# Forgetting attention and two MoE layers on one core: a new table of times for the order of the attention's operations and of the weight work between them

## The chip, the core and the metric

The kernel is one program on one core of a Trainium2 chip. The metric is the time of one execution on the device in microseconds (us); the median of several executions is compared. The core's engines work side by side, each on its own list of instructions in a fixed order: PE (TensorE, matrix products), DVE (VectorE), ACT (ScalarE), POOL (GpSimd), and SP (SyncE), whose queue issues most transfers. An instruction that waits holds up everything behind it on its own engine.

## What is computed

Three stages, each feeding the next; all data are fp32.

```python
# 32 heads (4 batches x 8 heads), S = 576 positions, D = 64
scores = (q @ k^T) / sqrt(D)
cum    = cumsum(log(clip(f, 1e-4, 1)))
scores = where(causal, -1e9, scores + cum[:, :, :, None] - cum[:, :, None, :])
attn   = exp(scores - max(scores)); attn = attn / (sum(attn) + 1e-9)
x      = attn @ v                             # to 2304 tokens x 512
x      = softplus(x @ w_in) @ w_out           # first MoE, 512 -> 2048 -> 512
out    = (sigmoid(x @ w_gate) * (x @ w_val)) @ w2_out   # second MoE, 512 -> 1536 -> 512
```

## The kernel before, in words

Products are made in fp32r from a high and a low half of each operand (three products for one), so copies to a high half and subtractions for a low half (names ending in `h` and `l`) follow nearly every step.

**Attention** works on 16 pairs of heads, `p` = 0 to 15. For one pair PE makes the scores: `s4` (tile `s{p}_4`, L225, all 128 rows) and `s3`, `s1`, `s2` (L239, two heads side by side on 64 rows each). DVE takes minimum and mask out of PSUM (`minimum`, L246), ACT makes the exponential and its sum (`exp`, L251). PE transposes the result in seven groups `t0` to `t6` (`transposes`, L270; two PSUM banks in turn), ACT copies each group out to its high half (`evac_h`, tile `PTh`, L292), DVE subtracts for the low half (`evac_l`, tile `PTl`, L296), and PE multiplies with the values (`pv`, L345) into an accumulator for each head, `x{p}_0` and `x{p}_1`, each one PSUM tile of 1024 columns. `pv(0, j)` stands for the j-th block of columns of the first head.

The sums go their own way: POOL adds the small constant (`rinv_a`, L301), DVE takes the reciprocal (`rinv`, L304), PE transposes the nine columns of it into the first 128 columns of the accumulator `x{p}_0` (`rinv_t`, L308), ACT copies these nine rows out (`rinv_b`, tile `rt_sb`, L312), SP writes them to DRAM and reads them back spread over rows (`rinv_c`, L316, tile `rd`; `rinv_d`, L322, tile `rb`). At the end ACT and DVE take the accumulators out (`out_a`, L355, tile `bs`; `out_b`, L360, tile `xs`), POOL multiplies with `rb` (`out_c`, L363), and SP writes the pair's result with three transfers (`out_d`, L370 to L372).

`Attention.run` sorts all operations of all pairs by one number each: 9 times the pair plus a number from the table WHEN (pair 0 takes START, pair 15 takes END). Engines keep that order; nothing else decides it. In the same sorted list stand the preparation of the first MoE's weights and its first work:

- STEPS and LATE_STEPS: steps of `Weights.op` by class. 0 LOAD (SP, L498, tile `raw`), 1 SCALE (ACT, L506, tile `w`), 2 SHIFT (DVE, L520), 3 LOW (DVE, L522), 4 SIGN (DVE, L524), 5 HI (ACT, L511), 6 LO (POOL, L514). The jobs are `wi0`, `wo0`, `wi1`, and so on.
- X_STEPS: loading the first 512 tokens (DVE L569, POOL L570), PRODUCTS: the first products `h0`, `h1` of the first MoE, UNITS: their softplus and split.

**The first MoE** then runs 80 units (5 token tiles x 16 blocks). A unit is PE's product `h` (12 matmuls, L577 to L579), ACT's softplus to `L` (L614) and copy to `gh` (L625), DVE's subtraction to `gl` (L626), and PE's product `o` (12 matmuls). One unit's `o` follows the next one's `h`. In the first tile each unit also ticks the weight chain on by two steps of each class.

Of the kernel before, what the change touches and what calls it, by code (L numbers as in the profile page):

```python
# [21 lines left out]
class Attention:  # L22
# [342 lines left out]
    def out_d(self, R, p):  # L365
# [13 lines left out]
        ("load_q",): 1.4836, ("qh",): 2.2896, ("load_k",): 3.0664, ("ql",): 3.3216, ("decay_rows",): 3.4423,  # L379
        ("kh",): 7.4598, ("kl",): 7.8752, ("scores", 4): 10.3002, ("load_v",): 11.0784, ("minimum", 4): 11.5052,  # L380
        ("scores", 3): 11.5060, ("minimum", 5): 14.0106, ("minimum", 3): 14.3071, ("scores", 1): 15.9948,
        ("minimum", 7): 16.2237, ("minimum", 1): 16.2736, ("minimum", 8): 16.3365, ("minimum", 0): 16.4858,
        ("exp", 4): 16.5320, ("exp", 5): 16.9077, ("scores", 2): 18.0750, ("exp", 3): 18.0806, ("exp", 7): 19.0711,
# [13 lines left out]
    START = {
        ("scores", 1): -280.1001, ("minimum", 7): -271.8782, ("minimum", 0): -231.7545, ("minimum", 8): -193.8316,
        ("minimum", 1): -187.7875, ("exp", 7): -173.7344, ("exp", 0): -167.8599, ("scores", 4): -157.5166,
        ("minimum", 4): -141.6254, ("scores", 2): -110.2675, ("exp", 4): -105.8996, ("minimum", 6): -105.0800,  # L400
        ("minimum", 2): -102.9800, ("scores", 3): -95.1511, ("exp", 6): -85.4990, ("exp", 2): -83.7134,
        ("exp", 8): -70.4444, ("exp", 1): -64.2521, ("minimum", 5): -59.3775, ("exp", 5): -50.7529,
        ("load_v",): -48.7810, ("transposes", 1): -35.9211, ("minimum", 3): -29.2582, ("exp", 3): -25.6744,
        ("transposes", 3): -19.5338, ("evac_h", 1): -8.3683, ("evac_h", 3): -6.7983, ("evac_l", 1): -1.6145,
        ("evac_l", 3): 10.5292, ("v_high",): 17.2888, ("rinv_a",): 18.4155, ("v_low",): 19.8820,
        ("transposes", 0): 20.3326, ("evac_h", 0): 21.2188, ("rinv",): 21.7400, ("evac_l", 0): 22.6562,
        ("transposes", 2): 22.8149, ("rinv_t",): 23.1362, ("evac_h", 2): 24.0607, ("rinv_b",): 24.3022,
        ("evac_l", 2): 24.5160, ("pv", 0, 0): 24.9295, ("transposes", 5): 24.9438, ("pv", 0, 2): 25.7706,
        ("transposes", 4): 25.7715, ("pv", 0, 4): 26.8567, ("evac_h", 5): 27.3271, ("evac_l", 5): 27.7081,
        ("evac_h", 4): 28.2950, ("evac_l", 4): 28.6956, ("transposes", 6): 28.8354, ("pv", 0, 3): 29.6197,  # L410
        ("rinv_c",): 29.8827, ("pv", 0, 1): 29.9362, ("evac_h", 6): 30.0612, ("evac_l", 6): 30.1210,
        ("pv", 1, 0): 30.1250, ("pv", 1, 2): 30.2412, ("out_a", 0): 32.2739, ("out_b", 0): 32.4826,
        ("rinv_d",): 33.9341, ("pv", 1, 4): 34.5831, ("pv", 1, 3): 35.1273, ("pv", 1, 1): 35.7267,
        ("out_a", 1): 36.1134, ("out_b", 1): 36.5534, ("out_c",): 40.4646, ("out_d",): 46.2880}
    END = {
        ("load_k",): -5.3504, ("load_q",): -2.6412, ("kh",): 3.0783, ("decay_rows",): 4.0312, ("qh",): 4.4239,
        ("load_v",): 4.8618, ("kl",): 5.5915, ("ql",): 7.9462, ("scores", 4): 10.6000, ("scores", 3): 11.4633,
        ("minimum", 4): 11.8140, ("minimum", 5): 13.7921, ("minimum", 3): 13.9946, ("exp", 4): 15.4472,
        ("exp", 5): 15.6399, ("scores", 1): 16.2743, ("minimum", 7): 16.8650, ("minimum", 1): 16.9709,
        ("exp", 1): 17.1448, ("minimum", 0): 17.2852, ("minimum", 8): 17.5873, ("exp", 0): 17.9416,  # L420
        ("exp", 8): 19.1832, ("scores", 2): 19.2862, ("v_high",): 19.8660, ("v_low",): 20.2468,
        ("minimum", 6): 20.6005, ("exp", 3): 21.0068, ("minimum", 2): 22.1762, ("exp", 7): 23.4705,
        ("exp", 6): 24.5954, ("exp", 2): 24.6233, ("transposes", 1): 24.7520, ("evac_h", 1): 24.7985,
        ("evac_l", 1): 25.3933, ("rinv_a",): 27.9027, ("transposes", 0): 29.1264, ("transposes", 3): 30.9396,
        ("evac_h", 0): 31.4482, ("evac_h", 3): 32.7310, ("evac_l", 0): 47.1260, ("rinv",): 56.8557,
        ("transposes", 2): 57.3718, ("evac_l", 3): 62.0535, ("transposes", 5): 63.6052, ("evac_h", 5): 77.8251,
        ("evac_h", 2): 79.9965, ("evac_l", 2): 85.0192, ("transposes", 4): 87.7824, ("rinv_t",): 92.6295,
        ("pv", 0, 0): 99.8173, ("evac_l", 5): 108.0667, ("transposes", 6): 108.0726, ("pv", 0, 4): 111.3911,
        ("pv", 0, 3): 111.7383, ("evac_h", 4): 113.9795, ("pv", 0, 2): 115.1968, ("evac_l", 4): 125.8108,
        ("evac_h", 6): 127.6254, ("pv", 0, 1): 132.0278, ("out_a", 0): 132.6996, ("rinv_b",): 152.9427,  # L430
        ("rinv_c",): 153.0347, ("evac_l", 6): 156.2053, ("pv", 1, 0): 166.3307, ("pv", 1, 3): 187.2979,
        ("pv", 1, 2): 201.4660, ("out_b", 0): 212.3156, ("pv", 1, 4): 218.5856, ("pv", 1, 1): 220.1616,
        ("rinv_d",): 225.0768, ("out_a", 1): 292.1891, ("out_b", 1): 319.5476, ("out_c",): 321.9904,
        ("out_d",): 353.5322}
# [543 lines left out]
LATE_STEPS = [(-16.2008, 2), (-15.8847, 5), (-14.7068, 3), (-12.1943, 6), (-3.5317, 1), (-3.1825, 0), (2.5760, 3),  # L978
              (13.9908, 4), (15.5227, 2), (26.5633, 5), (50.6610, 1), (56.3007, 3), (61.7718, 6), (69.1876, 2),
              (69.7883, 4), (72.7702, 3), (75.4909, 0), (90.6667, 0), (148.9901, 4), (149.6626, 0), (177.5320, 5),  # L980
              (208.1786, 4), (237.2145, 6), (441.5471, 0)]
X_STEPS = [-54.8771, -48.5972, -35.8360, -23.0657, -14.2717, -5.4128, -3.8231, 6.3816]
PRODUCTS = [43.6366, 61.7680]
UNITS = [100.4307, 349.1830]
# [198 lines left out]
```

## Time and profile before

| | us |
|---|---|
| median of 3 executions | 1013.31 (1012.34 to 1013.75) |
| profiled execution | 1011.11 |
| its span from first to last instruction | 1009.3 |
| PE busy | 1000.1 |
| DVE busy | 592.9 |
| ACT busy | 509.9 |
| POOL busy | 154.9 |

The profile is of one execution. Its span leaves out 1.8 us of the execution that stand before the first and behind the last instruction. PE is busy nearly all the time, so a microsecond that PE waits is close to a microsecond of time; where the other engines wait costs nothing by itself.

### The profile page before, as it was taken

Reading aid. Unit: us, or ns where it says so; the run is one execution under the profiler, and the core shown is the slowest. Engines: PE = TensorE matmul, PEld = TensorE weight load, DVE = VectorE, ACT = ScalarE, POOL = GpSimd, SP = SyncE. Lnnn points to the kernel's source line nnn. Section 1 sums busy time; section 2 is a strip of 40 time slices with the busy share of each in tenths; the row PEclk is TensorE's granted clock in tenths of the full one; section 3 lists DMA queues with packets and bytes.
Section 4 is the critical chain, followed back from the end, with each engine's and each line's share of the span. In section 5 each row is a group of like instructions: output and inputs, shape, how many; then the busy total and the mean of one; then the engine's idle time right before and its main releaser. Section 6 shows DMA issues by size and latency. Waiting matters only on the chain.

```text
span 1009.3 us, 15958 instructions
## 1 busy us (share of the span) xinstructions
PE 1000.1 (99%) x5614; PEld 883.9 (88%) x5614; DVE 592.9 (59%) x1210; ACT 509.9 (51%) x1085; POOL 154.9 (15%) x170
## 2 busy tenths in 40 slices
...
GB/s 176 162 162 161 165 164 132 108 156 207 208 64 207 251 260 205 182 177 168 238 83 248 226 185 338 212 247 214 219 269 209 248 223 208 188 265 216 217 137 63
DMA packets 114700, 196.10 MB, mean 194 GB/s; under 512 B 14702, under 2 KB 38398, under 8 KB 114620
## 3 DMA queue, kind: packets, MB, share of 16 engines
...
q8 instruction: 45, 0.74, 0.3%
...
## 4 chain that ended last, share of the span: by engine, by line
PE 91%; DMA 3%; DVE 2%; ACT 2%; POOL 1%; issue 1%; SPq 0%; POOLq 0%; ACTq 0%; DVEq 0%
PE z L577 9%; PE z L579 9%; PE z L578 9%; PE x L345 6%; PE h L577 6%; PE h L578 6%; PE h L579 6%; PE s L239 5%; PE t L270 5%; DMA raw_wo<-in_moe_w_out_dram 3%; PE oY L577 2%; PE oY L578 2%; PE oY L579 2%; PE s L225 2%; PE oX L577 2%; PE oX L578 2%
## 5 line engine op out<-in xcount | busy, mean ns | idle before, releaser
L577 PE MATMUL z<-three,three 128*128 128x384 f32 x456 | 153.3, 336 | 0.2
L579 PE MATMUL z<-three,three 128*128 128x384 f32 x456 | 152.9, 335 | 0.0
L578 PE MATMUL z<-three,three 128*128 128x384 f32 x456 | 152.6, 335 | 0.0
L626 DVE TENSOR_TENSOR gl<-L,gh 128x512 fp32r<-128x512 f32 (+1 forms) x80 | 51.1, 638 | 117.5 <-ACT gh L625 113.5
L614 ACT ACTIVATE L<-h 128x512 f32<-128x512 f32 (+1 forms) x80 | 44.3, 554 | 143.7 <-PE h L579 143.7
L577 PEld LDWEIGHTS z<-three,three 128*128 128x128 f32 x456 | 85.6, 188 | 2.7 <-DVE raw L887 0.5
L578 PEld LDWEIGHTS z<-three,three 128*128 128x128 f32 x456 | 85.6, 188 | 1.4
L251 ACT ACTIVATE P<-P,m 128x256 f32<-128x256 f32 (+3 forms) x144 | 83.7, 584 | 5.0 <-DVE m L246 4.7
L579 PEld LDWEIGHTS z<-three,three 128*128 128x128 f32 x456 | 85.6, 188 | 0.0
L246 DVE CUSTOM_DVE_ANT_0 P<-s,mask 128x256 f32<-128x256 f32 (+3 forms) x144 | 69.4, 515 | 10.6 <-PE s L239 9.4
L296 DVE TENSOR_TENSOR PTl<-t,PTh 128x512 fp32r<-128x512 f32 (+2 forms) x112 | 68.2, 619 | 5.4 <-ACT PTh L292 5.0
L874 ACT COPY bl<-z 128x384 f32<-128x384 f32 x36 | 17.3, 480 | 102.3 <-PE z L579 102.3
L886 DVE TENSOR_TENSOR raw<-z,bh 128x384 f32<-128x384 f32 x36 | 20.1, 558 | 76.5 <-PE z L579 76.5
L879 DVE TENSOR_TENSOR raw<-z,p 128x384 f32<-128x384 f32 x18 | 10.0, 558 | 92.9 <-PE z L579 79.0
L292 ACT CAST PTh<-t 128x512 fp32r<-128x512 f32 (+2 forms) x112 | 58.0, 539 | 9.5 <-PE t L270 7.0
L270 PE MATMUL t<-ident,P 128*128 128x128 f32 x400 | 61.9, 279 | 0.4 <-DVE PTl L296 0.4
L345 PE MATMUL x<-PTh,V 128*128 128x256 f32 (+2 forms) x224 | 59.1, 316 | 0.8 <-ACT rt_sb L312 0.8
L908 ACT CAST gh<-raw 128x384 fp32r<-128x384 f32 x72 | 33.5, 514 | 48.6 <-DVE raw L891 47.2
L345 PE MATMUL x<-PTl,V 128*128 128x256 f32 (+2 forms) x224 | 53.9, 292 | 0.0
L270 PEld LDWEIGHTS t<-ident,P 128*128 128x128 f32 x400 | 45.1, 140 | 7.6 <-DVE r L304 3.6
L727 DVE TENSOR_TENSOR l<-fw,sh 128x512 fp32r<-128x512 f32 x60 | 40.7, 687 | 13.9 <-ACT sh L726 7.1
L625 ACT CAST gh<-L 128x512 fp32r<-128x512 f32 (+1 forms) x80 | 46.2, 578 | 2.5
...
## 6 DMA issues: line engine op xcount, KB each, us to landing
...
```

The lines of the kernel that those rows point to most:

```text
L239: nc.tensor.matmul(ps[h][:, a:a + N], L[o], r[o, 0:N], start=j == 0, stop=j == n - 1)
L246: self.nc.vector.tensor_tensor_reduce(P, src, mask, -0.125, 3e38, op0=ALU.add, op1=ALU.min, accum_out=R["m"][:, t:t + 1])
L251: self.nc.scalar.activation(P, P, AF.Exp, bias=R["m"][:, t:t + 1], scale=-1.0, accum_out=R["sum"][:, t:t + 1])
L270: nc.tensor.transpose(ps[:, 128 * n:128 * n + 128], R["P"][:, o:o + 128], self.ident)
L292: self.nc.scalar.copy(d, s)
L296: self.nc.vector.tensor_sub(l, s, h)
L345: nc.tensor.matmul(R["acc%d" % h][:, o:o + n], v, t[:, col:col + n], start=j == 0 and w == 0, stop=j == 1 and w == 1)
L577: nc.tensor.matmul(ps, ah, bh, start=start and i == 0, stop=False, **how)
L578: nc.tensor.matmul(ps, ah, bl, start=False, stop=False, **how)
L579: nc.tensor.matmul(ps, al, bh, start=False, stop=stop and i == n - 1, **how)
L625: nc.scalar.copy(gh, s)
L626: nc.vector.tensor_sub(gl, s, gh)
```

## The change

Only numbers change: WHEN, START, END, STEPS, LATE_STEPS, X_STEPS, PRODUCTS, UNITS, the time at which the pools of the first MoE are opened, and that of the softplus table's preload. The operations, their sizes and their buffers are the same. Of the tables a few entries stand for all:

```diff
@@ WHEN (of 62 entries)
-        ("transposes", 0): 22.8649, ("transposes", 1): 23.1190, ("evac_h", 0): 23.3248, ("evac_l", 0): 23.4902,
...
-        ("evac_l", 4): 29.2931, ("evac_h", 6): 30.1251, ("evac_l", 6): 30.1452, ("pv", 0, 2): 30.2200,
-        ("pv", 0, 3): 30.6720, ("pv", 0, 1): 32.1361, ("pv", 1, 0): 32.9471, ("pv", 1, 2): 33.3019,
-        ("rinv_b",): 33.6120, ("out_a", 0): 34.7767, ("pv", 1, 4): 34.7925, ("pv", 1, 3): 35.3192,
...
+        ("transposes", 5): 29.8251, ("rinv_t",): 30.0728, ("pv", 0, 0): 30.1572, ("transposes", 4): 30.2737,
+        ("pv", 0, 4): 30.4394, ("rinv_b",): 30.4528, ("evac_h", 5): 30.5384, ("evac_l", 5): 30.6828,
...
+        ("evac_l", 6): 31.9050, ("rinv_c",): 32.2991, ("pv", 0, 3): 33.1511, ("pv", 0, 2): 34.6838,
@@ the list of other steps
-        others += [(end + 10.2872, open_pools), (end + 500, W.alone)]
+        others += [(end + 12.4572, open_pools), (end + 500, W.alone)]
...
-        others += [(end + 60.7767, lambda: nc.scalar.preload_act_table_set("softplus"))]
+        others += [(end + 73.1642, lambda: nc.scalar.preload_act_table_set("softplus"))]
```

What this does to the engines' lists is seen in the lists themselves. The first place is ACT in the middle of the attention, where pair 7's transposes are taken out (`t7_5`, `t7_4`) and pair 8's exponentials run (`P8`). Before:

```order
L292 CAST PTh_195<-t7_5_1747 128x2x256
L251 ACTIVATE P8_1579,sum8_1581<-P8_1579,m8_1580 128x256
L292 CAST PTh_195<-t7_4_1762 128x384
...
L292 CAST PTh_195<-t7_6_1790 128x2x128
...
L292 CAST PTh_195<-t8_0_1836 128x512
L292 CAST PTh_195<-t8_1_1842 128x512
L312 COPY rt_sb7_1871<-x7_0_1753 9x128
L251 ACTIVATE P9_1770,sum9_1772<-P9_1770,m9_1771 128x576
```

The same place in the changed kernel:

```order
L251 ACTIVATE P8_1605,sum8_1607<-P8_1605,m8_1606 128x256
L312 COPY rt_sb7_1789<-x7_0_1776 9x128
L292 CAST PTh_195<-t7_5_1770 128x2x256
L251 ACTIVATE P8_1605,sum8_1607<-P8_1605,m8_1606 128x256
L292 CAST PTh_195<-t7_4_1783 128x384
L251 ACTIVATE P8_1605,sum8_1607<-P8_1605,m8_1606 128x384
L292 CAST PTh_195<-t7_6_1816 128x2x128
```

The copy of `rt_sb` moved from behind the copies of the next pair's `t0` and `t1` to ahead of the copy of its own pair's `t5`. It does so in pairs 1 to 13; in pair 14, too, it now stands ahead of the copy of `t5`.

The second place is PE behind the scores `s3` of pair 9, with pair 7's products with the values (`x7_0`) and pair 8's transposes. Before:

```order
L239 MATMUL s9_3_1_1801<-nb1_133,one_135 128x512
L345 MATMUL x7_0_1753<-PTh_195,V7_1597 128x320
L345 MATMUL x7_0_1753<-PTl_196,V7_1597 128x320
L345 MATMUL x7_0_1753<-PTh_195,V7_1597 128x256
L345 MATMUL x7_0_1753<-PTl_196,V7_1597 128x256
L270 MATMUL t8_0_1836<-ident_184,P8_1579 128x128 x4
L270 MATMUL t8_1_1842<-ident_184,P8_1579 128x128 x4
```

And in the changed kernel:

```order
L239 MATMUL s9_3_1_1822<-nb1_133,one_135 128x512
L270 MATMUL t8_0_1836<-ident_184,P8_1605 128x128 x4
L270 MATMUL t8_1_1847<-ident_184,P8_1605 128x128 x4
L345 MATMUL x7_0_1776<-PTh_195,V7_1619 128x256
L345 MATMUL x7_0_1776<-PTl_196,V7_1619 128x256
L345 MATMUL x7_0_1776<-PTh_195,V7_1619 128x320
L345 MATMUL x7_0_1776<-PTl_196,V7_1619 128x320
```

The two groups of transposes moved ahead of four products with the values; all other PE instructions of a pair keep their places relative to one another.

The third place is ACT at the end of the attention, where the last pair's transposes (`t15_2`, `t15_4`, `t15_6`) and the first unit's softplus and copy (`L0`, `gh0`) stand. Before:

```order
L292 CAST PTh_195<-t15_2_3214 128x512
L614 ACTIVATE L0_3267<-h0_3200 128x512
L625 CAST gh0_3269<-L0_3267 128x512
L292 CAST PTh_195<-t15_4_3251 128x384
L292 CAST PTh_195<-t15_6_3264 128x2x128
L355 COPY bs15_3287<-x15_0_3255 64x576
L312 COPY rt_sb15_3289<-x15_0_3255 9x128
```

And in the changed kernel:

```order
L292 CAST PTh_195<-t15_2_3226 128x512
L312 COPY rt_sb15_3259<-x15_0_3219 9x128
L614 ACTIVATE L0_3261<-h0_3181 128x512
L625 CAST gh0_3263<-L0_3261 128x512
L292 CAST PTh_195<-t15_4_3251 128x384
L292 CAST PTh_195<-t15_6_3272 128x2x128
```

The last pair's copy moved to ahead of the first unit's softplus. SP's transfers follow it: the write of `rd15` moves ahead of the load of the weights `wo5`, the two reads of `rb15` ahead of the load of `wi6`. The three writes of pair 15's result still stand ahead of the load of `wo6` in both kernels. On DVE two weight steps of each pair now stand together behind the minimum of `s3` and ahead of the low half of `t0`; before they were spread over the pair.

## Rows read from the trace of the kernel before

**Rows 1.** Part 1 of the page: busy time, share of the span, instructions.
```profile
PE 1000.1 (99%) x5614; PEld 883.9 (88%) x5614; DVE 592.9 (59%) x1210; ACT 509.9 (51%) x1085; POOL 154.9 (15%) x170
```
**Rows 2.** Busy time of engines by window, in the middle of the attention; clock after POOL.
```profile
100.00:175.00 75.00, 75.00 (x629) 65.44 (x627) 69.92 (x200) 71.17 (x197) 62.37 (x59) 1.00 0.56 156
```
**Rows 3.** The chain of waits, pairs 2 and 7: start, us, what.
```profile
48.57 1.15 PE s L225 x8
...
101.74 0.90 PE s L239 x8
...
104.33 1.15 PE s L225 x8
```
**Rows 4.** Waits of PE: us in total, times, longest.
```profile
PE o L577 <- ACT gh L625: 1.7, 1, 1.7
...
PE x L345 <- ACT rt_sb L312: 0.8, 1, 0.8
PE o L578 <- DVE gl L626: 0.7, 3, 0.2
PE t L270 <- DVE PTl L296: 0.4, 1, 0.4
```
**Rows 5.** Timeline of ACT, pair 7's `t5` and `rt_sb` of pair 7.
```profile
103.32 0.59 ACT L292 CAST PTh<-t 128x512 fp32r<-128x512 f32 x1
...
109.00 0.26 ACT L312 COPY rt_sb<-x 9x128 f32<-9x128 f32 x1
```
**Rows 6.** Timeline of DVE: low half of `t5`, then a minimum of `s2`.
```profile
104.24 0.69 DVE L296 TENSOR_TENSOR PTl<-t,PTh 128x512 fp32r<-128x512 f32 x1
104.84 0.55 DVE L246 CUSTOM_DVE_ANT_0 P<-s,mask 128x384 f32<-128x384 f32 x1
```
**Rows 7.** Timeline of PE: `pv(0,4)`'s end, `t6`, `s3`, the next products.
```profile
104.06 0.28 PE L345 MATMUL x<-PTl,V 128*128 128x64 f32 x1
...
105.32 0.38 PE L270 MATMUL t<-ident,P 128*128 128x128 f32 x2
105.63 0.50 PE L239 MATMUL s<-Yh,Xh 64*128 64x512 f32 x2
...
106.20 0.39 PE L239 MATMUL s<-Yl,Xh 64*128 64x512 f32 x2
106.43 0.40 PE L239 MATMUL s<-nb,one 64*128 64x512 f32 x2
106.76 0.41 PE L345 MATMUL x<-PTh,V 128*128 128x320 f32 x1
```
**Rows 8.** Busy time by window, early in the first MoE.
```profile
214.00:218.00 4.00, 2.08 (x8) 1.21 (x7) 1.52 (x3) 3.00 (x6) 0.00 (x0) 0.99 0.59 239
218.00:222.00 4.00, 4.00 (x12) 3.08 (x12) 4.00 (x9) 3.31 (x6) 0.00 (x0) 0.58 0.11 10
```
**Rows 9.** Timeline of SP's queue: pair 15's `rd` and `rb`, load of `wo6`.
```profile
198.88 0.30 SPq L316 DMA_DIRECT2D rd<-rt_sb  x1
...
202.89 1.11 SPq L322 DMA_DIRECT2D rb<-rd  x2
...
210.34 0.60 SPq L498 DMA_DIRECT2D raw_wo<-in_moe_w_out_dram  x1
```
**Rows 10.** Timeline of ACT: `L0`, `rt_sb` of pair 15, scaling of `wo6`.
```profile
192.50 0.62 ACT L614 ACTIVATE L<-h 128x512 f32<-128x512 f32 x1
...
197.37 0.26 ACT L312 COPY rt_sb<-x 9x128 f32<-9x128 f32 x1
...
214.65 0.66 ACT L506 ACTIVATE w_wo<-raw_wo 128x512 f32<-128x512 f32 x1 [7.90 <-DMA raw_wo<-in_moe_w_out_dram]
```
**Rows 11.** Timeline of DVE: weight steps beside POOL and alone.
```profile
129.10 1.34 DVE L524 SCALAR_TENSOR_TENSOR w_wo<-raw_wo,w_wo 128x512 uint32<-128x512 uint32 x1
...
109.85 0.68 DVE L522 SCALAR_TENSOR_TENSOR w_wo<-raw_wo,w_wo 128x512 uint32<-128x512 uint32 x1
```
**Rows 12.** Timeline of POOL at the first of these.
```profile
128.31 1.59 POOL L184 TENSOR_TENSOR Xl<-qr,Xh 128x640 fp32r<-128x640 f32 x1
```

More of the change, by code (lines that the diff above doesn't have):

```diff
@@ L378 @@
     WHEN = {
[L379 to L383, printed above, removed]
@@ L384 @@
-        ("minimum", 2): 19.2572, ("minimum", 6): 19.3879, ("v_high",): 19.7353, ("exp", 0): 20.2360,
-        ("exp", 1): 20.6987, ("exp", 2): 21.1864, ("exp", 6): 21.4666, ("exp", 8): 21.9376,
-        ("transposes", 0): 22.8649, ("transposes", 1): 23.1190, ("evac_h", 0): 23.3248, ("evac_l", 0): 23.4902,
-        ("evac_h", 1): 23.6862, ("evac_l", 1): 23.6886, ("rinv_a",): 23.8842, ("v_low",): 24.3032,
-        ("transposes", 2): 25.4851, ("transposes", 3): 25.8584, ("evac_h", 2): 26.0442, ("evac_h", 3): 26.4650,
@@ L389 @@
-        ("evac_l", 2): 26.5420, ("rinv",): 26.6318, ("transposes", 5): 27.4187, ("evac_l", 3): 27.4813,
-        ("rinv_t",): 27.7344, ("pv", 0, 0): 27.8748, ("evac_h", 5): 28.0148, ("transposes", 4): 28.1460,
-        ("pv", 0, 4): 28.2287, ("evac_l", 5): 28.2585, ("evac_h", 4): 28.7290, ("transposes", 6): 28.8312,
-        ("evac_l", 4): 29.2931, ("evac_h", 6): 30.1251, ("evac_l", 6): 30.1452, ("pv", 0, 2): 30.2200,
-        ("pv", 0, 3): 30.6720, ("pv", 0, 1): 32.1361, ("pv", 1, 0): 32.9471, ("pv", 1, 2): 33.3019,
@@ L394 @@
-        ("rinv_b",): 33.6120, ("out_a", 0): 34.7767, ("pv", 1, 4): 34.7925, ("pv", 1, 3): 35.3192,
-        ("pv", 1, 1): 35.3392, ("out_b", 0): 35.4846, ("out_a", 1): 35.8332, ("out_b", 1): 36.9696,
-        ("rinv_c",): 39.2655, ("rinv_d",): 42.9840, ("out_c",): 46.3300, ("out_d",): 48.6884}
-    START = {
[L398 to L414, printed above, removed]
@@ L415 @@
-    END = {
[L416 to L434, printed above, removed]
@@ new lines @@
+        ("load_q",): -2.4386, ("load_k",): 1.3584, ("qh",): 3.5917, ("decay_rows",): 3.9289, ("ql",): 5.6054,
+        ("kh",): 9.2396, ("load_v",): 9.4014, ("kl",): 9.4265, ("scores", 4): 12.8748, ("minimum", 4): 13.5985,
+        ("scores", 3): 13.6410, ("minimum", 3): 14.4164, ("minimum", 5): 14.4817, ("exp", 4): 14.9535,
+        ("exp", 3): 16.5158, ("exp", 5): 17.8627, ("scores", 1): 18.5510, ("minimum", 1): 18.7579,
+        ("minimum", 8): 19.1186, ("minimum", 0): 19.3544, ("minimum", 7): 19.4831, ("exp", 0): 19.8260,
@@ new lines @@
+        ("scores", 2): 20.3431, ("exp", 1): 20.9919, ("minimum", 2): 21.1596, ("exp", 7): 21.5938,
+        ("minimum", 6): 21.7274, ("v_high",): 21.9880, ("exp", 2): 22.3252, ("transposes", 0): 23.4639,
+        ("exp", 6): 23.4684, ("transposes", 1): 24.1273, ("evac_h", 0): 24.4896, ("exp", 8): 24.5770,
+        ("rinv_a",): 24.7286, ("evac_h", 1): 25.3681, ("v_low",): 25.4076, ("evac_l", 0): 27.3390,
+        ("evac_l", 1): 27.5254, ("transposes", 2): 27.6644, ("transposes", 3): 28.2593, ("evac_h", 2): 28.7426,
@@ new lines @@
+        ("evac_h", 3): 28.9502, ("evac_l", 2): 29.2504, ("rinv",): 29.2519, ("evac_l", 3): 29.3724,
+        ("transposes", 5): 29.8251, ("rinv_t",): 30.0728, ("pv", 0, 0): 30.1572, ("transposes", 4): 30.2737,
+        ("pv", 0, 4): 30.4394, ("rinv_b",): 30.4528, ("evac_h", 5): 30.5384, ("evac_l", 5): 30.6828,
+        ("evac_h", 4): 30.7395, ("evac_l", 4): 30.8093, ("transposes", 6): 31.1825, ("evac_h", 6): 31.6647,
[3 rows of a table added]
+        ("rinv_d",): 38.0798, ("out_a", 1): 38.4245, ("out_b", 1): 38.7912, ("out_c",): 48.7607, ("out_d",): 51.4705}
@@ new lines @@
+    START = {
+        ("scores", 1): -309.9333, ("minimum", 8): -259.3040, ("minimum", 0): -243.4266, ("minimum", 1): -208.2944,
+        ("exp", 0): -194.7203, ("minimum", 7): -180.8479, ("scores", 4): -173.8326, ("exp", 7): -157.7781,
+        ("exp", 1): -156.2541, ("scores", 2): -148.0071, ("minimum", 4): -144.3496, ("minimum", 6): -136.7660,
+        ("exp", 8): -128.6214, ("minimum", 2): -110.4641, ("exp", 6): -110.2920, ("exp", 2): -99.0576,
+        ("exp", 4): -90.1841, ("scores", 3): -84.4027, ("minimum", 5): -62.3923, ("load_v",): -57.6412,
+        ("minimum", 3): -50.8286, ("exp", 5): -49.8013, ("transposes", 1): -45.2393, ("exp", 3): -36.5216,
+        ("evac_h", 1): -18.4625, ("transposes", 3): -8.3690, ("evac_h", 3): 2.6253, ("evac_l", 1): 4.2165,
+        ("evac_l", 3): 12.5054, ("v_high",): 18.7667, ("rinv_a",): 18.8621, ("v_low",): 19.1682, ("rinv",): 19.6605,
+        ("transposes", 0): 22.4752, ("evac_h", 0): 22.6272, ("evac_l", 0): 22.6912, ("transposes", 2): 22.8734,
+        ("rinv_t",): 23.8918, ("evac_h", 2): 24.5108, ("transposes", 5): 24.6953, ("rinv_b",): 24.8618,
+        ("evac_h", 5): 25.2001, ("pv", 0, 0): 26.2292, ("rinv_c",): 27.0299, ("evac_l", 2): 27.1715,
+        ("rinv_d",): 27.6621, ("pv", 0, 2): 27.7376, ("transposes", 4): 28.1234, ("pv", 0, 4): 28.4061,
+        ("evac_l", 5): 29.3320, ("evac_h", 4): 30.7400, ("transposes", 6): 31.1717, ("evac_l", 4): 31.4535,
[3 rows of a table added]
+        ("out_b", 1): 38.4750, ("out_c",): 44.8315, ("out_d",): 48.1512}
@@ new lines @@
+    END = {
+        ("load_k",): 0.4022, ("kh",): 2.5085, ("load_q",): 3.9124, ("qh",): 8.4646, ("ql",): 9.3031,
+        ("decay_rows",): 10.4439, ("kl",): 11.6954, ("load_v",): 11.9940, ("scores", 4): 12.5179,
+        ("scores", 3): 13.3287, ("minimum", 4): 13.7434, ("minimum", 5): 13.9165, ("minimum", 3): 14.3222,
+        ("exp", 4): 14.6129, ("exp", 5): 18.7059, ("scores", 1): 20.2055, ("minimum", 7): 20.8057,
+        ("exp", 3): 20.8780, ("minimum", 0): 21.1405, ("minimum", 1): 21.1948, ("minimum", 8): 21.3969,
+        ("scores", 2): 21.4562, ("exp", 1): 21.9054, ("exp", 7): 22.2752, ("minimum", 6): 22.4432,
+        ("minimum", 2): 23.0070, ("exp", 6): 24.7228, ("exp", 0): 24.8401, ("exp", 2): 27.4885,
+        ("transposes", 1): 27.5918, ("exp", 8): 27.6642, ("evac_h", 1): 27.8010, ("evac_l", 1): 28.3739,
+        ("transposes", 3): 29.0917, ("transposes", 0): 29.5384, ("v_high",): 29.6130, ("evac_h", 3): 31.2356,
+        ("evac_l", 3): 33.5022, ("rinv_a",): 38.7202, ("transposes", 5): 41.8339, ("rinv",): 47.8996,
+        ("evac_h", 0): 57.9792, ("evac_l", 0): 58.3751, ("rinv_t",): 69.1752, ("transposes", 2): 88.0664,
+        ("evac_h", 5): 90.0317, ("evac_h", 2): 94.0532, ("evac_l", 5): 94.2776, ("evac_l", 2): 96.1877,
+        ("v_low",): 107.8310, ("transposes", 4): 129.7428, ("pv", 0, 0): 136.5218, ("rinv_b",): 136.6238,
+        ("pv", 0, 3): 141.6982, ("transposes", 6): 151.3576, ("evac_h", 4): 155.1070, ("pv", 0, 4): 168.9115,
+        ("evac_l", 4): 172.2266, ("pv", 0, 2): 172.9962, ("rinv_c",): 188.4417, ("pv", 0, 1): 201.1722,
+        ("evac_h", 6): 202.2460, ("evac_l", 6): 205.8389, ("pv", 1, 0): 206.7900, ("out_a", 0): 215.9465,
+        ("rinv_d",): 233.4805, ("pv", 1, 4): 233.4991, ("out_b", 0): 238.3609, ("pv", 1, 3): 244.7150,
+        ("pv", 1, 2): 300.3282, ("pv", 1, 1): 307.2299, ("out_a", 1): 320.0174, ("out_b", 1): 329.3030,
+        ("out_c",): 333.5272, ("out_d",): 384.8411}
```

16 lines of the change are left out of this document (8 added, 8 removed), and 17 rows, old and new, of tables (START, STEPS, WHEN).

## The prediction

> **What bounds the kernel now.** The page's first part comes first: PE is busy for 1000.1 us [rows 1], so PE's own waits are nearly all there is to win, and any wait that an order puts in front of PE is added to the time. The windows then tell whether that holds stage by stage. In the middle of the attention PE is busy for all of 75 us, but DVE (69.92) and ACT (71.17) are nearly full too [rows 2]: the three engines run in step, each with little room. The chain of waits is PE's there, and the same piece, `s4`, comes at 48.57 and five pairs later at 104.33 [rows 3]: 55.76 / 5 = 11.15 us a pair. The list of what PE waits for is short [rows 4]: 1.7 us for `gh` (a single wait, in the first MoE), 0.8 for pair 0's `rt_sb`, 0.7 in three waits for `gl`, 0.4 once for a low half. The last views are the windows and timelines at 214 us, where a gap of PE and a low clock stand [rows 8 to 10].
>
> **What the change removes, adds and moves.** No operation is added or removed; each term is a wait gained or lost.
>
> *The copy of `rt_sb` in pairs 1 to 13.* The copy reads nine rows of the accumulator `x{p}_0`, which `rinv_t` has written, but `pv(0,0)` and `pv(0,4)` of the same pair write the same tile and stand between them in the order. Does the copy wait for those products? The row for it is pair 0's wait: there PE's product with the values waited 0.8 us for `rt_sb` [rows 4], though the product writes other columns than the copy reads. So the tile is guarded as a whole, and I take it that it is guarded in the other direction too. In the old place the guard cost nothing: at 109.00 [rows 5] the products of pair 7 had passed. In the new place it does. The last of `pv(0,4)` ends at 104.06 + 0.28 = 104.34 [rows 7]. Behind the waiting copy on ACT stands the high half of `t5`, which before began at 103.32 and took 0.59 [rows 5]. Now: copy from about 104.37, the next instruction some 0.16 later (0.26 less the overlap of 0.1 that neighbours show in [rows 6]), high half to 105.12, low half on DVE 0.69 [rows 6], to 105.85. `t6` goes into the bank that `t5` leaves, so it starts at about 105.88 instead of 105.32 [rows 7]: 0.56 us. What covers it on PE is `s4` alone, 1.15 us [rows 3], and it is used up in this sum. The minimum of `s2` stands behind that low half on DVE and frees a bank of `s3`: 105.76 + 0.55 [rows 6] = 106.31. `s3` would stand ready 0.31 behind `t6` [rows 7], at 106.19, and so waits about 0.16 more. Together 0.72 a pair, 13 x 0.72 = 9.4 us. Bounds: 0 if the copy waits only for `rinv_t`, 0.9 if ACT needs longer to start. Behind that, DVE and ACT are late by less than PE, and the longer period gives both more room, so I add nothing there.
>
> *Pair 14.* The same copy, with `s2` (0.90 [rows 3]) as cover instead of `s4` (1.15) and no `s3` behind it: 0.56 + 0.25 = 0.8 us.
>
> *Pair 15.* The copy now stands ahead of `L0` and `gh0` and waits for `pv(0,0)`, which stands behind the product `h1` on PE. Queued behind it are `L0` (0.62 [rows 10]), `gh0` (about as long) and the high half of `t4`; PE's next product waits for the copy as in pair 0, and `pv(0,1)` for both halves of `t4`. An estimate: 0.4 for the copy, 0.5 until the high half, 1.1 until the low half, which has `gl0` and a weight step ahead of it on DVE: 2.0 us. Bounds 0.5 and 3.
>
> *Transposes ahead of products.* Going from the 64-row scores of `s3` to a product costs PE a step of 0.33 (106.43 to 106.76) where one within the scores costs 0.23 (106.20 to 106.43) [rows 7]. Now transposes follow `s3`, and the products follow transposes. At most that 0.10 is saved, if the passage into transposes is free; at least nothing. I take 0.05 a pair, 14 x 0.05 = 0.7 us gained.
>
> *Start and end of the attention.* In pair 0 four transposes now stand between `rinv_t` and the first product: they hide about 0.45 of the 0.8 us [rows 4]. The one wait of 0.4 for a low half [rows 4] stands in pair 14's old order and goes.
>
> *The first MoE.* Before, the load of `wo6` was issued at 210.34 [rows 9], because it stands in SP's queue behind the three writes of pair 15's result, which need `rb15`; that came late because `rt_sb15` was copied at 197.37 [rows 10], written at 198.88 and read back from 202.89 [rows 9]. ACT then waited 7.90 us for `wo6` with `L3` behind it [rows 10], and PE for `gh3` [rows 4]. The windows show the loss: 4.00 - 2.08 = 1.92 us idle, then 4.00 us at a granted clock of 0.58 of the 2.4 GHz level, some of it at the lower level: 4.00 x 0.42 = 1.68 [rows 8]. Now `rt_sb15` comes about 1.2 us behind `h1` instead of 3.2, and `rb15` is read ahead of the load of `wi6`. With PE itself 2 us later, `wo6` is issued some 6 us earlier against PE than before. The gap was 1.9, so it closes, and with it goes the stretch of low clock: 3.6 us, plus 0.6 of the later waits for `gl` (0.7 [rows 4]): 4.2 gained. Bounds: 0 if pair 15's writes still hold `wo6` back, 5.
>
> *Weight steps on DVE.* They now stand in twos ahead of `t0`'s low half. I cost them at nothing: `t2` on PE needs the bank of `t0` more than 1 us later than DVE would leave it, by the sums above, and 1 us is what covers them. If a step is held by POOL, that cover goes; this is the second rival.
>
> The sum: 9.4 + 0.8 + 2.0 - 0.7 - 0.45 - 0.4 - 4.2 = +6.5 us. Against the profiled execution's own 1011.1 that is 1017.6. The median of the runs shown is 2.2 us higher than that execution, so for the median I give 1013.3 + 6.5 = 1019.8.
>
> **The rivals.** *Faster: the copy does not wait for the products.* If the guard on the accumulator is only for the columns read, ACT copies `rt_sb` 0.9 us earlier, the 9.4 and the 0.8 go, and so does most of the 2.0. What is left is -0.7 - 0.45 - 0.4 - 4.2 = -5.75: 1007.6. For it speaks that only `rinv_t` writes the columns that are copied; against it pair 0's wait. Between the two lies the point from which it decides: with the rest as above, (5.75 - 2.8) / 13 = 0.23 us a pair. A wait of about that size, since ACT and DVE might make good part of the delay, would leave the time where it was.
>
> *Slower than forecast: POOL holds DVE's weight steps.* A step of this kind takes 0.68 alone [rows 11] and took 1.34 at 129.10, while POOL's subtraction ran from 128.31 to 129.90 [rows 11, 12]; DVE's step ended 0.54 behind POOL's. In the new order the second weight step of a pair comes when POOL's low half of V may start, 1.6 us long. If POOL gets in first, `t0`'s low half is late by some 1.7, of which about 1 is covered: 0.7 in some 9 pairs is 6.3 us, 1026. For it speaks that both want to start within 0.3 us; against it that POOL's short `rinv_a` stands ahead of the low half and that a slower pair shifts them apart. The Trainium skill (SBUF — State Buffer, section "Who interferes with whom") says that a VectorE instruction with two inputs in SBUF contends with a GpSimd one that reads SBUF, that the loser is blocked for the whole instruction, and that the order of issue decides who loses; the row of 1.34 us agrees. By that rule alone the steps would cost 0 or the 6.3, with nothing between.
>
> *The transition's gain fails.* If the load of `wo6` is still late by over 6 us, or the waits of pair 15 bring a stretch of low clock of their own, the 4.2 go: 1024.
>
> **How the numbers follow.** Chances: the forecast 0.55, with a range of its own of 1016 to 1023; the copy without a wait 0.18; POOL holding DVE 0.12; the transition's gain lost 0.08; a partly covered copy wait that leaves the time alone 0.07. The forecast is that of the likeliest, 1019.8. The range of 8 in 10 reaches from the faster rival, 1007, to the POOL rival, 1026, since cases of both signs hold a good part of the chance. A measurement of this kernel tells a change from none at about 0.2%, that is 2 us: faster 0.18, same 0.08, slower 0.74.
>
> **What the changed profile would show.** If I am right, `s4` comes every 11.8 us instead of 11.15; the list of PE's waits has a row for `t6` on the low half of `t5` (about 0.5 us, 13 times) and one for `s3` on a minimum; on ACT `rt_sb` starts just as `pv(0,4)` ends, behind idle time put down to PE. At the end of the attention PE waits about 2 us on `rt_sb`, `PTh` and `PTl` of pair 15, and there is no wait for `gh3` and no window of clock 0.58 behind it. Wrong is the main step if the period is 11.1 and `rt_sb` starts ahead of `pv(0,4)`'s end; wrong is the transition if ACT waits for `wo6` again; the DVE step is wrong if weight steps of 1.3 us stand ahead of `t0`'s low half and PE waits at `t2`.

## The result: slower by 0.56%

The changed kernel takes 1017.91 us (median of 6 executions, 1016.55 to 1020.52); the kernel before took 1012.77 beside it (6 executions, 1010.96 to 1013.75). The ratio is 1.0056, with a 95% interval of 1.0045 to 1.0067: slower, by 5.1 us between the medians. The two profiled executions stand 1017.55 to 1011.11, and their spans 1015.8 to 1009.3, 6.5 us apart.

The page's first part, for the changed kernel. PE does 1.1 us more by its modelled ends [rows 1] in a span that is 6.5 us longer: what is new is waiting, not work.

```profile
PE 1001.2 (99%) x5614; PEld 884.5 (87%) x5614; DVE 591.6 (58%) x1210; ACT 508.9 (50%) x1085; POOL 154.2 (15%) x170
```

What PE of the changed kernel waits for (us in total, times, longest), where [rows 4] stood before:

```profile
PE t L270 <- DVE PTl L296: 5.5, 14, 0.4
...
PE o L577 <- ACT gh L625: 1.0, 1, 1.0
PE x L345 <- DVE PTl L296: 0.9, 1, 0.9
PE x L345 <- ACT rt_sb L312: 0.7, 2, 0.4
```

Fourteen waits of transposes for a low half are new, against one of 0.4 before. In the first MoE the wait for `gh` lost 0.7 of its 1.7, and pair 15 brought a wait of 0.9. The list counts only idle time behind the modelled end of the product before; what a wait costs in all is read from the stretches at the end of this section.

Now one pair. First PE's timeline: the first product of `s4` of pair 4, five pairs later the last product of `pv(0,4)` and the next `s4`, then `t6` and `s3`, where [rows 7] stood.

```profile
48.67 0.38 PE L225 MATMUL s<-Yh,Xh 128*128 128x288 f32 x1
...
107.69 0.28 PE L345 MATMUL x<-PTl,V 128*128 128x64 f32 x1
107.80 0.38 PE L225 MATMUL s<-Yh,Xh 128*128 128x288 f32 x1
...
109.51 0.44 PE L270 MATMUL t<-ident,P 128*128 128x128 f32 x2 [0.41 <-DVE PTl L296]
109.88 0.60 PE L239 MATMUL s<-Yh,Xh 64*128 64x512 f32 x2
```

ACT in the same microsecond (answers to [rows 5]):

```profile
108.00 0.25 ACT L312 COPY rt_sb<-x 9x128 f32<-9x128 f32 x1 [1.04 <-PE x L345]
108.16 0.57 ACT L292 CAST PTh<-t 128x512 fp32r<-128x512 f32 x1
```

And DVE (answers to [rows 6]):

```profile
108.77 0.69 DVE L296 TENSOR_TENSOR PTl<-t,PTh 128x512 fp32r<-128x512 f32 x1 [0.82 <-ACT PTh L292]
109.38 0.55 DVE L246 CUSTOM_DVE_ANT_0 P<-s,mask 128x384 f32<-128x384 f32 x1
```

The reader is to see one delay handed on three times. The last `pv(0,4)` ends at 107.69 + 0.28 = 107.97. The copy of `rt_sb`, for which ACT had been idle 1.04 us, starts at 108.00. It reads columns 0 to 127 of the accumulator, and `pv(0,4)` writes columns 768 to 831 of the same tile. The high half of `t5` follows, DVE waits 0.82 for it, and PE waits 0.41 for the low half at `t6`. `s4` comes every (107.80 - 48.67) / 5 = 11.83 us, before 11.15.

Pair 15 and the load of `wo6`, on SP's queue (answers to [rows 9]):

```profile
203.96 0.28 SPq L316 DMA_DIRECT2D rd<-rt_sb  x1
...
205.18 1.12 SPq L322 DMA_DIRECT2D rb<-rd  x2
...
214.12 0.60 SPq L498 DMA_DIRECT2D raw_wo<-in_moe_w_out_dram  x1
```

On ACT (answers to [rows 10]):

```profile
203.68 0.25 ACT L312 COPY rt_sb<-x 9x128 f32<-9x128 f32 x1 [2.93 <-PE x L345]
...
218.14 0.68 ACT L506 ACTIVATE w_wo<-raw_wo 128x512 f32<-128x512 f32 x1 [1.65 <-DMA raw_wo<-in_moe_w_out_dram]
```

And the windows there (answers to [rows 8]); the granted clock is the number behind POOL's:

```profile
212.00:216.00 4.00, 4.00 (x19) 3.34 (x18) 2.10 (x4) 2.57 (x6) 0.30 (x1) 1.00 0.49 99
216.00:220.00 4.00, 4.00 (x19) 3.30 (x19) 3.71 (x7) 1.17 (x2) 0.00 (x0) 1.00 0.27 105
```

The load of `wo6` comes 5.1 us behind the first `o` (which starts at 208.98), before 12.0 (198.31 to 210.34). ACT waits 1.65 us for it instead of 7.90, PE has no gap, and its clock stays full.

The starts on PE's timeline, put side by side, give the whole sum by stretch:

| from, to | before | after | difference | foretold |
|---|---|---|---|---|
| start to `s4` of pair 3 | 37.25 | 36.81 | -0.44 | -0.45 |
| to `s4` of pair 15 (12 pairs) | 133.88 | 142.08 | +8.20 | 12 x 0.67 = +8.0 |
| to `h1` | 20.07 | 20.90 | +0.83 | 0.67 + 0.8 - 0.4 = +1.1 |
| to the first `o` | 7.11 | 9.19 | +2.08 | +2.0 |
| to `h3` | 8.17 | 8.20 | +0.03 | 0 |
| `h3` to `h20` | 98.12 | 94.31 | -3.81 | -4.2 |
| `h20` to the last matmul's end | 700.98 | 700.53 | -0.45 | 0 |

### The profile page after: what moved, and what is told of

The parts are those of the page before. It is cut to its first block, busy times and chain, and to the rows that moved or that the text cites. A ratio compares the mean times of both kernels' runs of the same rounds, so it can differ in the third digit from the quotient of the medians.

```text
span 1015.8 us, 15949 instructions
## 1 busy us (share of the span) xinstructions
PE 1001.2 (99%) x5614; PEld 884.5 (87%) x5614; DVE 591.6 (58%) x1210; ACT 508.9 (50%) x1085; POOL 154.2 (15%) x170
## 4 chain that ended last, share of the span: by engine, by line
PE 91%; ACT 3%; DVE 3%; DMA 2%; POOL 1%; issue 1%; POOLq 0%; ACTq 0%; SPq 0%; DVEq 0%
PE z L577 9%; PE z L579 9%; PE z L578 9%; PE h L579 6%; PE h L577 6%; PE h L578 6%; PE t L270 5%; PE x L345 5%; PE s L239 5%; PE oY L579 2%; PE oY L578 2%; PE oY L577 2%; PE oX L579 2%; PE oX L578 2%; PE oX L577 2%; PE o L578 2%
## 5 line engine op out<-in xcount | busy, mean ns | idle before, releaser
L251 ACT ACTIVATE P<-P,m 128x128 f32<-128x128 f32 (+3 forms) x144 | 84.0, 584 | 7.1 <-DVE m L246 5.2
L345 PE MATMUL x<-PTh,V 128*128 128x320 f32 (+2 forms) x224 | 57.5, 310 | 0.9 <-ACT rt_sb L312 0.7
L345 PE MATMUL x<-PTl,V 128*128 128x320 f32 (+2 forms) x224 | 54.4, 292 | 0.9 <-DVE PTl L296 0.9
```

The lines of the kernel that those rows point to most:

```text
L251: self.nc.scalar.activation(P, P, AF.Exp, bias=R["m"][:, t:t + 1], scale=-1.0, accum_out=R["sum"][:, t:t + 1])
L345: nc.tensor.matmul(R["acc%d" % h][:, o:o + n], v, t[:, col:col + n], start=j == 0 and w == 0, stop=j == 1 and w == 1)
```

## The experiments

Numbers are medians, with the lowest and highest execution where they matter, and ratios to the kernel before that ran beside each.

**1. The copy back to its old place, all else new.** In WHEN:

```diff
-        ("pv", 0, 4): 30.4394, ("rinv_b",): 30.4528, ...
-        ("evac_l", 6): 31.9050, ("rinv_c",): 32.2991, ...
+        ("rinv_b",): 35.0200, ("rinv_c",): 35.0300   # behind ("pv", 0, 1): 35.0048
```

> The changed kernel with one thing put back: in pairs 1 to 14 the copy of rt_sb stands behind pv(0,1) again, as before. Theory (the copy waits for pv(0,4) and holds t5, t6 and s3 back, 13 pairs by 0.7 us and pair 14 by 0.8): s4 comes every 11.1 us, some 10 us less than the changed kernel, about 1008, below the kernel before. Rival (the longer period comes from the weight steps in twos on DVE, or from transposes ahead of products): the period stays at 11.8 and the time at about 1018.

1008.15 us (1006.37 to 1011.40), ratio 0.9949 (0.9933 to 0.9964): 9.8 us under the changed kernel, and faster than the kernel before. The chain of waits shows the period: (103.92 - 48.10) / 5 = 11.16, and 11.13 in the last pairs.

```profile
48.10 1.15 PE s L225 x8
...
92.79 1.15 PE s L225 x8
103.92 1.15 PE s L225 x8
```

The copy's place alone makes the change slow; the weight steps in twos and the order of transposes and products cost nothing that shows. The rest of the new order is worth some 4.5 us.

**2. The copy's new place alone, in the kernel before.**

```diff
-        ("rinv_b",): 33.6120, ("evac_h", 5): 28.0148
+        ("rinv_b",): 28.2288, ("evac_h", 5): 28.2289   # behind ("pv", 0, 4): 28.2287
```

> The kernel before with one thing of the change: the copy of rt_sb behind pv(0,4) and ahead of the high half of t5, in pairs 1 to 14. Theory: period 11.85 instead of 11.15, 10 us more than before, about 1023, and a wait of t6 on the low half of t5 in each pair. Rival: the period stays at 11.15, because the copy finds room in the old order of ACT and DVE, and the time at about 1013.

1021.79 us, ratio 1.0087 (1.0071 to 1.0103), 9 us slower, with 16 waits of transposes for a low half:

```profile
PE t L270 <- DVE PTl L296: 6.7, 16, 0.6
```

`s4` comes every 11.87 us, where 11.85 was foretold. One copy moved (the high half of `t5` gets a new number only to stay behind it), and the loss is there. With the run before it this settles the main step from both sides.

**3. The copy ahead of `pv(0,0)` in the order, at the same place of ACT's list.**

```diff
-        ("rinv_b",): 30.4528   # behind ("pv", 0, 4)
+        ("rinv_b",): 30.1000   # ("rinv_t",): 30.0728, ("pv", 0, 0): 30.1572
```

> The changed kernel with the copy of rt_sb in program order ahead of pv(0,0) instead of behind pv(0,4); ACT's list is the same as in the changed kernel. Theory (the accumulator is guarded as one tile, whichever comes first in the order waits not): the copy starts when rinv_t ends, about 0.9 us earlier, the wait for t6 goes, and now pv(0,0) waits for the copy, about 0.55 us a pair: period 11.65, some 2 us less than the changed kernel, 1016. Rival (only the columns that are copied are guarded): no wait at pv(0,0) and period 11.1, 1008.

1016.65 us, ratio 1.0036 (1.0024 to 1.0049). The wait changes sides, as a guard on the whole tile says. ACT's copy is released by `rinv_t` (L308) now, and PE's product waits for it. PE's timeline:

```profile
107.38 0.27 PE L308 MATMUL x<-ident,r 128*9 128x128 f32 x1
108.09 0.36 PE L345 MATMUL x<-PTh,V 128*128 128x256 f32 x1 [0.44 <-ACT rt_sb L312]
```

ACT's timeline at the same moment:

```profile
107.69 0.26 ACT L312 COPY rt_sb<-x 9x128 f32<-9x128 f32 x1 [0.20 <-PE x L308]
```

PE waits 6.3 us on it in 14 pairs (in the changed kernel 0.7 in two), and `s4` comes every 11.75 us, where 11.65 was foretold. A guard on columns alone would have given no wait at all, so that rival is out.

**4. The same, with `rinv_t` ahead of `t5` on PE.**

```diff
+        ("rinv_t",): 29.8200, ("rinv_b",): 30.1000   # ahead of ("transposes", 5): 29.8251
```

> As the run before, and rinv_t ahead of the transposes of t5, so that these stand between rinv_t and pv(0,0). Theory: the copy is done while PE makes t5 (0.44 us and its passage), pv(0,0) waits at most 0.1: period 11.1 to 11.2, 1008 to 1009.5, as good as putting the copy late. Rival: rinv_t itself waits for the reciprocal, and half of the gain is lost, 1012.

1014.17 us, ratio 1.0006 (0.9997 to 1.0015): 3.7 us under the changed kernel where experiment 1 has 9.8, and not for the reason that either side named. `rinv_t` ran early enough, ending at 104.93 + 0.28 = 105.21, but ACT was in an exponential then. ACT's timeline:

```profile
104.91 0.51 ACT L251 ACTIVATE P<-P,m 128x256 f32<-128x256 f32 x1
...
105.42 0.24 ACT L312 COPY rt_sb<-x 9x128 f32<-9x128 f32 x1
```

PE's timeline:

```profile
104.93 0.28 PE L308 MATMUL x<-ident,r 128*9 128x128 f32 x1
105.04 0.60 PE L270 MATMUL t<-ident,P 128*128 128x128 f32 x4
105.81 0.50 PE L345 MATMUL x<-PTh,V 128*128 128x256 f32 x2 [0.16 <-ACT rt_sb L312]
```

The expectation had counted the copy from the end of `rinv_t` and left out what stands ahead of it on ACT.

**5. Experiment 1, and pair 15's copy back as well.** In END `("rinv_b",)` from 136.6238 to 216.5 and `("rinv_c",)` from 188.4417 to 216.6.

> The first experiment (late copy in pairs 1 to 14), and pair 15's copy also put back to behind the first head's accumulator copy, where it stood before. Theory: the 2 us of waits at pair 15 (copy, then t4's high and low half) go; rb15 comes later against PE, but still early enough for the load of wo6, so nothing comes back: about 1006, 2 us below the first experiment. Rival: with rb15 late the wait for wo6 and the low clock come back, 3.6 us, and the time is about 1010.

1009.86 us (1008.14 to 1011.27), ratio 0.9963 (0.9950 to 0.9977): no gain on experiment 1. Two things stand against the theory. `h1` to the first `o` takes 8.37 us, in experiment 1 it took 9.21 and before 7.11: only 0.84 goes when the copy moves, and a wait of 1.10 for the low half of `t4` stays. And though the load of `wo6` did no harm where it did before, the loss came back later: 0.25 of waiting for `gh` at 254 and 1.46 at 267, with a low clock behind it.

```profile
264.00:268.00 4.00, 2.54 (x11) 1.62 (x9) 1.42 (x3) 2.68 (x6) 0.00 (x0) 1.00 0.70 265
268.00:272.00 4.00, 3.77 (x12) 2.87 (x12) 4.00 (x9) 1.72 (x5) 0.00 (x0) 0.66 0.00 1
```

**6. Experiment 1, and pair 15's copy just behind the high half of `t4`.** In END `("rinv_b",)` from 136.6238 to 155.2, behind `("evac_h", 4)`: 155.107.

> The first experiment, and pair 15's copy behind the high half of t4, so that L0, gh0 and t4 go ahead of it, and pv(0,4) waits for it. Theory: the waits for t4's halves (0.2 and 0.9) go, the one for the copy stays or grows by some tenths, the load of wo6 stays early: 1.0 to 1.5 us below the first experiment, about 1007.

1006.86 us (1006.07 to 1007.76), ratio 0.9938 (0.9925 to 0.9950): 1.3 under experiment 1, the size foretold, though the two intervals overlap, and 6 us under the kernel before. The reason came only in part: of the waits that were to go, 0.71 for the low half of `t4` is left. On DVE a SHIFT step that took 1.50 (0.42 elsewhere) stands ahead of it in an unbroken row of instructions, the likely cause; no run removed that step. First PE's timeline, then DVE's:

```profile
196.92 0.41 PE L345 MATMUL x<-PTl,V 128*128 128x320 f32 x1 [0.71 <-DVE PTl L296]
```

```profile
193.70 1.50 DVE L520 TENSOR_SCALAR w_wo<-w_wo 128x512 uint32<-128x512 uint32 x1
```

**7. The old WHEN and START with all else new.** The two tables of the kernel before, in the changed kernel.

> The tables WHEN and START of the kernel before with all else of the changed kernel: the last pair, the weight steps and the first units in their new order, pairs 0 to 14 in the old one. Theory: period 11.15; from the kernel before 4 us less in the first MoE and 2 us more at pair 15, 1010.5. Rival (the weight steps' new places cost by themselves, POOL holding DVE): period above 11.3 and no gain, 1013 or more.

1024.55 us, ratio 1.0112 (1.0098 to 1.0126): slower than anything else here. From pair 3 on `s4` comes every 11.15 to 12.6 us. Before 175 us five of DVE's LOW and SIGN steps take 0.96 to 1.80 us instead of 0.68 (two in the kernel before, one in the changed kernel). One of the five on DVE's timeline, and then the longest waits of PE:

```profile
122.02 1.80 DVE L524 SCALAR_TENSOR_TENSOR w_wo<-raw_wo,w_wo 128x512 uint32<-128x512 uint32 x1
```

```profile
PE t L270 <- DVE PTl L296: 5.2, 7, 1.7
PE s L225 <- POOL Yl L184: 2.3, 1, 2.3
PE s L239 <- DVE m L246: 2.0, 3, 1.0
```

The rival's mechanism is real; how much of the 12 us it makes was not taken apart. More of the loss lies behind the pairs than in them: from `s4` of pair 3 to that of pair 15 PE takes 140.38 us (133.88 before), from there to `h1` 30.13 (20.07 before), where the old numbers of pair 14 meet the new END. One side of it is clean: with PE this late, `h3` to `h20` takes 92.48 us, that is 17 units of 5.44, without a wait.

**8. The load of `wo6` ahead of pair 15's writes, alone in the kernel before.** In LATE_STEPS:

```diff
-              (208.1786, 4), (237.2145, 6), (441.5471, 0)]
+              (208.1786, 4), (237.2145, 6), (340.0000, 0)]
```

> The kernel before with one number changed: the load of wo6 stands in SP's queue ahead of the three writes of pair 15's result. Theory (the wait of ACT for wo6, PE's gap of 1.9 us and the low clock behind it all come from this place in the queue): the load is issued at about 204 instead of 210.3, ACT's wait for it and the window of clock 0.58 are gone, 3.6 us less, 1009. Rival (the weights come too slowly anyway, and the wait only moves to wi7 or wo7): gain under 1.5 us, 1011.5 or more.

1009.96 us (1007.81 to 1012.43), ratio 0.9970 (0.9958 to 0.9982): 2.9 us less. The load is issued at 205.84, and the windows of [rows 8] are full at full clock:

```profile
214.00:218.00 4.00, 4.00 (x20) 3.30 (x19) 3.07 (x6) 1.10 (x2) 0.00 (x0) 1.00 0.72 265
218.00:222.00 4.00, 4.00 (x19) 3.20 (x18) 2.59 (x6) 3.65 (x8) 0.00 (x0) 1.00 0.61 249
264.00:268.00 4.00, 2.59 (x11) 1.71 (x10) 1.46 (x3) 2.65 (x5) 0.00 (x0) 1.00 0.75 262
```

So the place in SP's queue is the cause of the gap at 214. The third line is what the rival had seen: a wait of 1.41 for `gh` comes at 267 instead. In the profiled executions most of the gain is lost again that way: from `h4` to `h5`, where the gap was, PE takes 5.44 us instead of 9.52, but from `h3` to `h20` still 97.31 instead of 98.12.

**9. Experiment 6, with the tokens' step behind the softplus in each unit of the first MoE.**

```diff
+        self.hidden(u, pieces)
         if 0 <= k < 8 and t + 1 < self.NT:
             self.x.step(t + 1, k)
-        self.hidden(u, pieces)
```

> The sixth experiment, and in each unit of the first MoE the step that loads or copies the next tile's tokens stands behind the unit's softplus and weight steps instead of ahead of them. Theory on the waits that were left behind unit 10 (in the sixth experiment the profile shows 1.25 us of ACT on the tokens' transfer with the softplus queued behind it, then PE 0.49 on gh): they come from this place in ACT's list, go with it, and with them the occasional low clock: 0.7 to 2 us below the sixth experiment, 1005 to 1006. Rival: the weight chain itself is slower than PE, ACT waits the same on the weights, and the time stays at 1007.

1005.68 us (1005.27 to 1007.25), ratio 0.9926 (0.9910 to 0.9941). It has the lowest median of all, 7.4 us under the kernel before. It does not settle the cause: its interval overlaps experiment 6's, and its profile has a wait of 0.36 for `gh` left (0.49 there), now with ACT idle 2.38 us on a weight's transfer:

```profile
255.70 0.69 ACT L506 ACTIVATE w_wi<-raw_wi 128x512 f32<-128x512 f32 x1 [2.38 <-DMA raw_wi<-in_moe_w_in_dram]
```

**10. Experiment 9, with the low half of pair 15's `t4` ahead of a weight step on DVE.** In END `("evac_h", 4)` to 140.0 and `("evac_l", 4)` to 141.0.

> The ninth experiment, and at pair 15 both halves of t4 ahead of the weight step that stood in front of the low half on DVE. Theory on what is left of pair 15's waits (in the sixth experiment 0.71 us of PE on the low half of t4): DVE makes a weight step of 0.68 ahead of it, and the wait falls to 0.1 or less; the time falls by 0.6, to about 1005, which the medians may not tell apart. Rival: the step ahead of that one (SHIFT, 1.50 us beside POOL instead of about 0.42) is the cause, and the wait stays above 0.4.

1007.83 us (1006.05 to 1008.33), ratio 0.9952 (0.9938 to 0.9965): no gain. The wait for `t4` went, and a wait of 1.0 for the low half of `t6` came, since the weight step that was passed now meets POOL's `LO` step and takes 1.58. DVE's timeline, then POOL's:

```profile
195.69 0.55 DVE L296 TENSOR_TENSOR PTl<-t,PTh 128x384 fp32r<-128x384 f32 x1
196.16 1.58 DVE L522 SCALAR_TENSOR_TENSOR w_wo<-raw_wo,w_wo 128x512 uint32<-128x512 uint32 x1
197.66 0.41 DVE L296 TENSOR_TENSOR PTl<-t,PTh 128x256 fp32r<-128x256 f32 x1
```

```profile
195.91 1.28 POOL L514 TENSOR_TENSOR wo_l<-w_wo,wi_h 128x512 fp32r<-128x512 f32 x1 [1.02 <-ACT wi_h L511]
```

In experiment 9 the same step took 0.68 at its old place.

## Why the prediction was right

**The sum.** +6.5 us was foretold, and the profiled executions differ by 6.4. The medians differ by 5.1 only, and the base of the forecast, 1013.3, was 0.5 above the 1012.77 measured beside the changed kernel; so 1019.8 stands 1.9 above 1017.91. That the sum fits so well is in part luck: the first MoE gave 0.4 less than foretold, and the stretch behind `h20` gave 0.45 that no term had.

**The copy of `rt_sb`.** Right in kind and in size: 0.67 net a pair was foretold, 8.20 / 12 = 0.68 came. Experiments 1 and 2 take it away and make it; the copy's start 0.03 behind the end of `pv(0,4)` and the wait that changes sides in experiment 3 show that the whole tile is guarded, both ways. Its parts hold too. From `s4` to `t6` PE takes 1.71 us in the changed kernel (107.80 to 109.51) and 1.15 before and in experiment 1, 0.56 more, as foretold. From `t6` to the end of `s3` it takes 0.15 more than in experiment 1 (0.06 to its start, 0.09 within it), 0.16 was foretold. The cause given for these, a minimum that frees the bank late, fits but is not shown: the minimum ends at 109.38 + 0.55 = 109.93, beside the start of `s3` at 109.88, and the row of `s3` waiting for a minimum that was foretold is not in the list of waits.

**Pair 14 and the end of the attention.** The stretch gave +0.83 instead of +1.1. Experiment 1 takes it apart: without the copy the stretch is 19.99, so the copy costs 0.91 there (0.72 + 0.8 = 1.5 foretold), and all else gains 0.08 on 20.07, not the 0.4 of the old wait.

**Pair 15.** Right in size (2.08 for 2.0) and, in the changed kernel, in its chain. The waits are 0.34 for the copy, 0.16 for the high half of `t4` and 0.90 for the low half, 1.4 in all where 0.4, 0.5 and 1.1 were foretold; the other 0.7 of the stretch is no wait of the list and was not read. DVE of the changed kernel shows the chain: `gl0` waits for `gh0`, which stands behind the copy, and `gl0` and a weight step of the usual 0.68 stand ahead of the low halves of `t4` and `t6`.

```profile
205.11 0.69 DVE L626 TENSOR_TENSOR gl<-L,gh 128x512 fp32r<-128x512 f32 x1 [1.73 <-ACT gh L625]
205.72 0.68 DVE L522 SCALAR_TENSOR_TENSOR w_wo<-raw_wo,w_wo 128x512 uint32<-128x512 uint32 x1
206.32 0.88 DVE L296 TENSOR_TENSOR PTl<-t,PTh 128x384 fp32r<-128x384 f32 x2
```

What the prediction did not see is a second delay behind the first. When the copy is moved back only 0.84 is gained, for in experiments 5 and 6 the SHIFT step beside POOL now stands ahead of the same low half, and in experiment 10 a LOW step ahead of that of `t6`. That is the mechanism of the second rival, in another place.

**The first MoE.** The gap at 214 and the low clock behind it went, by the place of `rt_sb15` and `rb15` in the queues: experiment 8 moves one load, and the gap goes as well. The gap was worth 4.08 (`h4` to `h5` took 9.52 instead of 5.44), 3.6 foretold. The small part of the term was wrong: 0.6 of later waits was counted as gained, but these cost 1.56 before and 1.83 in the changed kernel, where a wait of 1.0 for `gh` stands. Between `h3` and `h20` PE alone needs 92.48 us; the kernel before lost 5.64 there, the changed one 1.83, experiment 6 1.29, experiment 8 4.83, experiment 5 5.67. What is saved early is in part lost again some 50 us later. That PE then catches up with the weights is not shown: PE reaches `h3` at 207.03, 207.17, 207.82 and 207.90 in experiments 5, 6, 10 and 1, and the profiled executions lose 5.67, 1.29, nothing and 4.36. What limits the weights there stays open.

**Start and transposes.** The start gave -0.44 for -0.45. Of the 0.05 a pair taken for transposes ahead of products, experiment 1 leaves 0.02: 11.13 against 11.15.

**The rivals.** The copy without a wait is out by the changed kernel's own trace and by experiment 3, and with a cost of 0.68 a pair the partly covered wait is out too. The transition's gain did not fail: ACT waits 1.65 us for `wo6`, but PE has no gap there. POOL holding DVE in the middle of the attention did not come: the changed kernel has a single LOW or SIGN step over 0.9 us before 175, at 123.13, and the period there is 12.03 instead of 11.8.

## What to carry to other kernels

In this program a small copy out of an accumulator waits for everything that has been ordered into that tile before it, whatever columns it reads; put it where that is long done, and count what stands behind it on its engine. Ahead of the first product, with something else for PE in between, it gave back only 3.7 of 9.8 us here. A step that moves in an order has three neighbours: what it waits for, what is queued behind it, and what that in turn releases; the price is the last of these less the cover there. A wait removed early in a pipeline can come back later in the same stage, as in experiment 8; read its worth from the whole stage.

## What had not been expected

Pair 15's `rd` is a transfer of 4.6 KB, and `rb` reads it back. In the kernel before 4.0 us pass between the two issues (198.88 to 202.89), with two loads of weights of 512 KB issued just ahead of it; in the changed kernel 1.2 us (203.96 to 205.18), with one such load 3.4 us ahead of it. In experiment 5 it is again 1.2 (198.18 to 199.41), in experiment 8 5.4 (199.19 to 204.63), where the loads stand as before. In experiments 1 and 6, with a load 1.8 and 2.0 us ahead, it is 2.0 and 1.9. So the small transfer took longer the closer behind a load it was issued; since no run moved the loads alone, that they are the cause is not shown.

The first MoE's later wait may vary from one execution to the next; with one profile for each kernel this is not shown. Experiment 1's executions spread over 5 us, and its profiled one, the slowest, has a wait of 1.54 for `gh` at 267 and this window behind it:

```profile
268.00:276.00 8.00, 8.00 (x29) 6.42 (x30) 5.90 (x11) 3.41 (x7) 0.00 (x0) 0.79 0.38 131
```

At a granted clock of 0.79, some 1.7 of these 8 us are lost, an estimate (8 x 0.21). A wait for `gh` was followed by a stretch at the lower level (1.2 GHz) in some profiled executions (1.70 before, 1.54 in experiment 1, 1.46 in experiment 5) and not in others (1.41 in experiment 8, 1.47 at 281 in experiment 2, 0.99 in the changed kernel).
